# The last mixer of a three-part kernel: low parts, normalisation and the root chain placed on other engines

## Chip, cores and metric

The kernel runs on one core of a Trainium2 chip. The metric is device time of one execution in microseconds (us), taken as the median of several executions. The engines are named as the profile names them: PE (TensorE matmul, with its weight loads as PEld), DVE (VectorE), ACT (ScalarE), POOL (GpSimd) and SP (the queue that issues the DMAs).

## What is computed

The reference is a chain of three parts on a tensor of 4 batches, 768 positions and 384 features: a delta-rule attention, then a Fourier mixing with an MLP, then a gated mixer. Only the last part is touched by the change:

```python
def _moe2_ref(x, w_in, w_spatial, b_spatial, w_out):
    h = np.maximum(x @ w_in, 0.0)
    d_ff = h.shape[-1]
    u, v = (h[..., :d_ff // 2], h[..., d_ff // 2:])
    mu = np.mean(v, axis=-1, keepdims=True)
    var = np.mean((v - mu) ** 2, axis=-1, keepdims=True)
    v_n = (v - mu) / np.sqrt(var + 1e-06)
    v_s = np.einsum('ts,bsd->btd', w_spatial, v_n) + b_spatial[None, :, None]
    gated = u * v_s
    return (gated @ w_out).astype(np.float32)
```

## The kernel before, in words

Everything is float32 in and out. TensorE reads its operands as fp32r, which keeps fewer bits, so each operand is split into a high part (a rounded copy, made by ScalarE) and a low part (source minus high part). A product is then three matmuls: high by high, high by low, low by high (`PASS`).

The gated mixer is `mlp2`, and it works batch by batch, four times. In one batch:

- **Block stage.** Three blocks `kk` of positions. For each, two tiles of `v` (128 positions by 512, `v0` and `v1`, one from each half of the sequence) come from 9 matmuls each (L964); ScalarE applies the relu from PSUM (L967), VectorE takes mean and variance (L968, L969). A chain on two numbers per row (L970 to L976) makes the reciprocal of the deviation: add 1e-6, a root on ScalarE (L971), one Newton step that refines that root, a reciprocal. L978 normalises both tiles. The spatial product is done in the Winograd form of Strassen's method, seven products of half size for four, so VectorE also builds four sums of quarter tiles (L983 to L986, `S`). `operands` makes the high (L947, ScalarE) and low (L948, GpSimd) part of each: per block one of 256 elements per row and three of 512, all into the tile `A`.
- **Left halves.** Eight tiles `u` of 128 by 384, 9 matmuls each (L995), relu by ScalarE (L999). TensorE does these 72 matmuls while the block stage's last block is still being worked on.
- **Spatial products.** Seven products for each of two column halves `m`, 9 matmuls each (L1015), in a bank of PSUM each. VectorE adds their results up from PSUM (L1018 to L1034). `gate` multiplies a result by its `u` (L1002), ScalarE makes the high part (L1004), GpSimd the low part (L1005).
- **Output.** 72 matmuls with `wo` (L1043), a copy from PSUM by ScalarE (L1049), a store.
- Beside the products, the next batch is turned to its transposed form (`turn`): VectorE transposes 32x32 blocks into the scratch `x[0]` (L754), SP issues 16 small DMAs, and ScalarE and VectorE split the result (L745, L746). The scratch is one region, so the second half's L754 waits until the first half's 16 DMAs have landed.

`L964`'s tiles, the `u` tiles and the spatial products share one set of four PSUM banks, `bankX`. A bank comes free when ScalarE (L967, L999) or VectorE (L1018 to L1034) has read it.

The order on each engine isn't written by hand in this stage: a list scheduler with its own model of durations sets it when the kernel is built, and each engine then works strictly in that order. So an instruction that waits holds up everything behind it on its engine.

Of the kernel before, what the change touches and what calls it, by code (L numbers as in the profile page):

```python
# [7 lines left out]
F32 = mybir.dt.float32  # L8
F32R = mybir.dt.float32r
I32 = mybir.dt.int32  # L10
AF = mybir.ActivationFunctionType
ALU = mybir.AluOpType
AX = mybir.AxisListType
SUB, ADD, MUL, MAX = ALU.subtract, ALU.add, ALU.mult, ALU.max
# [3 lines left out]
DM = H * D  # L18
# [47 lines left out]
class Kernel:  # L66
# [863 lines left out]
    def mlp2(self, prep, x, wi, Bo, wo, bsb, A, hs, p, sm, out):  # L930
        nc = self.nc
        xs = x[0].rearrange("p t f -> p (t f)")
        vs = [xs[:, 0:DG], xs[:, DG : 2 * DG]] + [hs[:, i * DG : i * DG + DG] for i in range(4)]
        S = xs[:, 2 * DG : 4 * DG].rearrange("p (o c) -> p o c", o=4)
        tmp = [hs[:, i * DM : i * DM + DM] for i in range(6)]
        ots = [xs[:, (3 + i) * DM : (4 + i) * DM] for i in range(3)]

        gl = [A[:, 0, o].rearrange("p h k c -> p (h k c)") for o in (0, 3, 4, 1)]
        bias = [bsb[:, i * DM : i * DM + DM] for i in range(2)]
        n_out = 0  # L940

        def operands(at, n, kk, src):

            o = A[:, :, at : at + n, :, kk]
            hi, lo = (o[:, :, :, i].rearrange("p m o c -> p o m c") for i in range(2))
            src = src.rearrange("p (o m c) -> p o m c", o=n, m=2)
            nc.scalar.copy(out=hi, in_=src)  # L947
            nc.gpsimd.tensor_sub(lo, src, hi.bitcast(F32))  # L948

        for b in range(B):  # L950
            for got in prep:
                pass
            xT = got
            prep = self.mlp2_prep(x[b + 1], lambda: xs[:, : 3 * DM]) if b + 1 < B else iter(())
            for kk in range(3):
                q = sm[:, kk % 2]
                st, mv = q[:, :12].rearrange("p (t n) -> p t n", t=2), q[:, 12:16].rearrange("p (t n) -> p t n", t=2)
                v, s, r = (q[:, 16 + 2 * i : 18 + 2 * i] for i in range(3))
                v0, v1 = vs[2 * kk : 2 * kk + 2]
                for t, vt in enumerate((v0, v1)):  # L960
                    pv = self.bank("h", [128, DG])
                    for c in range(3):
                        for j, (i, k) in enumerate(PASS):
                            nc.tensor.matmul(  # L964
                                pv, lhsT=xT[t][i][:, c, kk * 128 : kk * 128 + 128], rhs=wi[2 * c + 1][k], start=(c + j == 0), stop=(c == 2 and j == 2)
                            )
                    nc.scalar.activation(vt, pv, AF.Relu)  # L967
                    nc.vector.bn_stats(out=st[:, t], in_=vt)  # L968
                    nc.vector.bn_aggr(out=mv[:, t], in_=st[:, t])  # L969
                nc.vector.tensor_scalar_add(v, mv[:, :, 1], 1e-6)  # L970
                nc.scalar.sqrt(s, v)  # L971
                nc.vector.reciprocal(r, s)
                nc.vector.tensor_mul(v, v, r)
                nc.vector.tensor_add(v, v, s)
                nc.vector.tensor_scalar_mul(v, v, 0.5)
                nc.vector.reciprocal(r, v)  # L976
                for t, vt in enumerate((v0, v1)):
                    nc.vector.tensor_scalar(out=vt, in0=vt, scalar1=mv[:, t, 0:1], scalar2=r[:, t : t + 1], op0=SUB, op1=MUL)  # L978
                    if t == 0:
                        operands(0, 1, kk, v0[:, :256])  # L980
                    else:
                        operands(1, 2, kk, v1)
                nc.vector.tensor_add(S[:, 0], v0[:, 256:], v1[:, 256:])  # L983
                nc.vector.tensor_sub(S[:, 1], S[:, 0], v0[:, :256])
                nc.vector.tensor_sub(S[:, 2], v0[:, :256], v0[:, 256:])
                nc.vector.tensor_sub(S[:, 3], v1[:, :256], S[:, 1])  # L986
                for i in range(2):
                    operands(3 + 2 * i, 2, kk, xs[:, (2 + i) * DG : (3 + i) * DG])
            u, gh = {}, {}
            for hf in range(2):  # L990
                for f in range(4):
                    pu = self.bank("h", [128, DM])
                    for c in range(3):
                        for j, (i, k) in enumerate(PASS):
                            nc.tensor.matmul(  # L995
                                pu, lhsT=wi[2 * c][i][:, f * 128 : f * 128 + 128], rhs=xT[hf][k][:, c], start=(c + j == 0), stop=(c == 2 and j == 2)
                            )
                    u[hf, f] = p.tile([128, DM], F32, name=f"u{hf}{f}")
                    nc.scalar.activation(u[hf, f], pu, AF.Relu)  # L999

            def gate(g, f, hf):
                nc.vector.tensor_mul(g, g, u[hf, f])  # L1002
                gh[hf, f] = p.tile([128, DM], F32R, name=f"u{hf}{f}")
                nc.scalar.copy(out=gh[hf, f], in_=g)  # L1004
                nc.gpsimd.tensor_sub(gl[f][:, hf * DM : hf * DM + DM], g, gh[hf, f].bitcast(F32))  # L1005

            for m in range(2):
                t1, t2, t5, t3 = (tmp[i] for i in ((0, 1, 2, 3), (4, 5, 0, 1))[m])
                add = nc.vector.tensor_add

                def product(o, name):
                    acc = self.bank("h", [128, DM])
                    for kk in range(3):
                        for j, (i, k) in enumerate(PASS):
                            nc.tensor.matmul(acc, lhsT=A[:, m, o, i, kk], rhs=Bo[name, kk][:, k], start=(kk + j == 0), stop=(kk == 2 and j == 2))  # L1015
                    return acc

                add(t1, product(0, "11"), bias[0])  # L1018
                add(t2, product(4, "T2"), t1)
                add(t5, product(3, "T1"), bias[1])  # L1020
                if m:
                    got = next(prep, None) or got
                add(t1, product(1, "21"), t1)
                gate(t1, m, 0)
                add(t3, product(5, "T3"), t2)
                add(t2, t2, t5)
                add(t5, t3, t5)
                gate(t5, 2 + m, 1)
                got = next(prep, None) or got
                add(t2, product(6, "22"), t2)  # L1030
                gate(t2, m, 1)
                if m:
                    got = next(prep, None) or got
                add(t3, product(2, "T4"), t3)  # L1034
                gate(t3, 2 + m, 0)
                if m == 0:
                    got = next(prep, None) or got

            def result(po, t, hf, fs, last):
                for f in fs:  # L1040
                    for j, (i, k) in enumerate(PASS):
                        a = gl[f][:, hf * DM + t * 128 :] if i else gh[hf, f][:, t * 128 :]
                        nc.tensor.matmul(po, lhsT=a[:, :128], rhs=wo[f][k], start=(f + j == 0), stop=(f == last and j == 2))  # L1043

            def store(po, t, hf):
                nonlocal n_out
                o = ots[n_out % 3]
                n_out += 1
                nc.scalar.copy(out=o, in_=po)  # L1049
                self.load(out=out[6 * b + 3 * hf + t], in_=o)  # L1050

            po = [self.bank("o", [128, DM]) for _ in range(3)]
            for t in range(3):
                result(po[t], t, 1, (0, 2, 3), 1)
                got = next(prep, None) or got
            for t in range(3):
                result(po[t], t, 1, (1,), 1)
                store(po[t], t, 1)
            for t in range(3):
                po = self.bank("o" if t else "pz", [128, DM])  # L1060
                result(po, t, 0, (0, 2, 1, 3), 3)
                store(po, t, 0)
# [269 lines left out]
```

## Time and profile before

| | |
|---|---|
| median of 3 executions | 870.35 us (868.94 to 871.19) |
| the profiled execution, its own time | 869.52 us |
| its span from first to last instruction | 867.7 us |
| busy share: PE, DVE, ACT, POOL | 96%, 74%, 47%, 12% |
| granted TensorE clock over the span | 0.984 of full speed |
| `mlp2`: from the first L964 to the last matmul | 616.3 to 864.4 us |
| POOL instructions of L948 and L1005 | 48 and 32 |

The stage that the change touches is the last 29% of the span. There the granted clock is 1.00 throughout, TensorE is busy nearly all the time, and the useful reading is where TensorE stops and for whom. A matmul's shown duration runs past the start of the next, since matmuls overlap: work per matmul is the distance from start to start, not the duration. Idle time in brackets is what an engine had no instruction running, with the engine, tile and line that ended it.

### The profile page before, as it was taken

How to read it: one execution, taken by the hardware profiler on the slowest of the kernel's cores; microseconds unless marked ns; L12 is line 12 of the kernel's file. 1: busy time of each engine (PE TensorE's matmuls, PEld its weight loads, DVE VectorE, ACT ScalarE, POOL GpSimd, SP SyncE). 2: the span in 40 equal slices, each digit the busy share in tenths (PEclk: the TensorE clock that was granted, in tenths of full speed). 3: DMA queues.
4: the chain of work that ended last, by engine and by line, in shares of the span. 5: the costliest groups of instructions: out<-in, count | busy, mean ns of one | idle time of the engine just before them, and what ended most of it. 6: DMA issues, size and time to landing. Idle time of an engine off the chain costs nothing.

```text
span 867.7 us, 18516 instructions
## 1 busy us (share of the span) xinstructions
PE 836.4 (96%) x7147; PEld 805.1 (93%) x7147; DVE 645.0 (74%) x1828; ACT 405.0 (47%) x991; POOL 101.5 (12%) x109
## 2 busy tenths in 40 slices
PE   7979999999998899999999999999999999999998
PEld 7869999999998798999999999999989889999998
DVE  4999999998968897785664892426698487667672
ACT  1669888889765434222213352224442432423432
POOL 2000000000000000000000000000063253333351
PEclk8969999999999999999999999999999999999999
DMA  8275665533550900001022411112001101102001
GB/s 222 67 189 135 172 189 161 160 84 104 141 168 20 341 5 1 1 2 28 1 69 78 128 28 28 37 55 64 29 0 49 62 9 47 56 25 62 25 1 54
DMA packets 57675, 67.21 MB, mean 77 GB/s; under 512 B 31826, under 2 KB 48947, under 8 KB 57587
## 3 DMA queue, kind: packets, MB, share of 16 engines
q1 hardware_dynamic: 57586, 66.03, 26.4%
q8 instruction: 56, 0.92, 0.5%
q14 instruction: 33, 0.26, 0.1%
HBM read 53.62 MB, written 4.72 MB: 67 GB/s over the span
## 4 chain that ended last, share of the span: by engine, by line
PE 70%; DVE 22%; ACT 3%; DMA 2%; issue 2%; SPq 1%; POOL 0%; DVEq 0%; ACTq 0%; POOLq 0%
PE bankX L818 15%; PE bankY L831 14%; PE bankX L1015 8%; PE bankY L1043 5%; PE bankY L438 3%; PE bankY L409 3%; PE bankY L440 3%; PE bankY L425 3%; PE bankX L964 3%; PE bankX L221 2%; DVE tm L308 2%; DVE Ts L313 2%; PE bankX L637 2%; PE bankZ L380 2%; PE bankV L831 1%
## 5 line engine op out<-in xcount | busy, mean ns | idle before, releaser
L831 PE MATMUL bankY<-w,hx 128*128 128x384 f32 x756 | 149.0, 338 | 2.2 <-DVE w L720 1.2
L818 PE MATMUL bankX<-uh,w 128*128 128x384 f32 x504 | 136.2, 337 | 0.7 <-DVE ul L746 0.7
L831 PEld LDWEIGHTS bankY<-w,hx 128*128 128x128 f32 x756 | 132.3, 188 | 3.9 <-DVE w L720 1.8
L823 DVE SCALAR_TENSOR_TENSOR hx<-bankX,hx 128x384 fp32r<-128x384 f32 x84 | 46.2, 551 | 72.8 <-ACT hx L822 72.5
L822 ACT ACTIVATE hx<-bankX 128x384 fp32r<-128x384 f32 x84 | 41.2, 490 | 126.2 <-PE bankX L818 121.8
L948 POOL TENSOR_TENSOR A<-x,A 128x512 fp32r<-128x512 f32 (+1 forms) x32 | 40.2, 1277 | 485.5 <-ACT A L947 485.5
L818 PEld LDWEIGHTS bankX<-uh,w 128*128 128x128 f32 x504 | 91.6, 188 | 1.3 <-DVE ul L746 0.9
L1015 PE MATMUL bankX<-w,A 128*128 128x384 f32 x456 | 82.9, 335 | 2.7 <-ACT u L999 2.7
L818 PE MATMUL bankX<-ul,w 128*128 128x384 f32 x252 | 84.5, 335 | 0.0
L1015 PEld LDWEIGHTS bankX<-w,A 128*128 128x128 f32 x456 | 79.3, 188 | 3.6 <-ACT u L999 3.6
L438 PE MATMUL bankY<-WU,gak 128*112 128x96 f32 (+1 forms) x384 | 70.1, 271 | 2.7 <-ACT x L455 2.7
L440 PE MATMUL bankY<-Sb,cw 112*112 112x96 f32 (+1 forms) x352 | 64.2, 265 | 2.6 <-DVE cw L426 2.5
L313 DVE TENSOR_TENSOR Ts<-Ts,tm 128x110 f32<-128x110 f32 (+26 forms) x264 | 59.4, 263 | 0.9
L308 DVE TENSOR_TENSOR tm<-Ts 128x110 f32<-128x110 f32 (+26 forms) x264 | 59.0, 261 | 0.4
L438 PEld LDWEIGHTS bankY<-WU,gak 128*112 128x112 f32 (+1 forms) x384 | 52.2, 178 | 5.9 <-ACT x L455 3.4
L409 PE MATMUL bankY<-gak,TT 128*128 128x96 f32 x384 | 53.1, 284 | 4.4 <-ACT gak L402 4.0
L414 ACT COPY WU<-bankY 64x384 f32<-64x384 f32 x96 | 45.4, 473 | 21.7 <-PE bankY L409 20.3
L409 PEld LDWEIGHTS bankY<-gak,TT 128*128 128x128 f32 x384 | 49.8, 203 | 5.1 <-ACT gak L402 4.4
L440 PEld LDWEIGHTS bankY<-Sb,cw 112*112 112x112 f32 (+1 forms) x352 | 48.4, 176 | 3.9 <-issue 2.1
L995 PE MATMUL bankX<-xh,s 128*128 128x384 f32 x192 | 49.6, 336 | 0.0
L1004 ACT CAST u<-hx 128x384 fp32r<-128x384 f32 x32 | 16.0, 513 | 67.4 <-DVE hx L1002 67.4
L818 PEld LDWEIGHTS bankX<-ul,w 128*128 128x128 f32 x252 | 47.3, 188 | 0.0
(217 smaller groups left out, 1781.6 us busy)
## 6 DMA issues: line engine op xcount, KB each, us to landing
kq<-in_kq_dram SPq DMA_DIRECT2D x24, 448.0 KB, 3.9
qt<-in_qt_dram SPq DMA_DIRECT2D x48, 196.0 KB, 3.4
gak<-in_kv_dram SPq DMA_DIRECT2D x48, 192.0 KB, 3.8
w<-in_w_dram SPq DMA_DIRECT2D x24, 384.0 KB, 7.8
out_dram<-x SPq DMA_DIRECT2D x24, 192.0 KB, 1.9
kq<-in_kc_dram SPq DMA_DIRECT2D x8, 448.0 KB, 12.7
x<-x SPq DMA_DIRECT2D x96, 36.0 KB, 1.9
s<-in_wi_dram SPq DMA_DIRECT2D x6, 512.0 KB, 4.4
```

Of the source, the lines that this page charges most:

```text
L308: nc.vector.tensor_tensor(out=tm, in0=T[:, r, k : k + 1].to_broadcast(sh), in1=T[:, k : k + 1, :k].to_broadcast(sh), op=MUL)
L313: nc.vector.tensor_add(o, o, tm)
L409: nc.tensor.matmul(pb[:, hp].rearrange("p t d -> p (t d)"), lhsT=tt[:, o + hp], rhs=kv[:, hp], start=True, stop=True)
L414: nc.scalar.copy(out=o_, in_=pb[hs])
L438: nc.tensor.matmul(pd[:m, hp], lhsT=ak[:, hp, :m], rhs=u[:, hp], start=True, stop=(c == 0))
L440: nc.tensor.matmul(pd[:m, hp], lhsT=cw[:, hp, :m], rhs=sb[:, hp], start=False, stop=True)
L818: nc.tensor.matmul(ph, lhsT=w1[f][i][:, c * 128 : c * 128 + 128], rhs=cur[k][:, c], start=(c + j == 0), stop=(c == 2 and j == 2))
L823: nc.vector.scalar_tensor_tensor(out=hl, in0=ph, scalar=0.0, in1=hh.bitcast(F32), op0=MAX, op1=SUB)
L831: nc.tensor.matmul(acc[t], lhsT=hx[i][:, t * 128 : t * 128 + 128], rhs=w2[e][k], start=(e == 0 and j == 0), stop=(e == 11 and j == 2),)
L995: nc.tensor.matmul(pu, lhsT=wi[2 * c][i][:, f * 128 : f * 128 + 128], rhs=xT[hf][k][:, c], start=(c + j == 0), stop=(c == 2 and j == 2))
L1015: nc.tensor.matmul(acc, lhsT=A[:, m, o, i, kk], rhs=Bo[name, kk][:, k], start=(kk + j == 0), stop=(kk == 2 and j == 2))
L1043: nc.tensor.matmul(po, lhsT=a[:, :128], rhs=wo[f][k], start=(f + j == 0), stop=(f == last and j == 2))
```

## The change

Four edits, all in `mlp2`. Line numbers after the second edit are one higher than before, so L1015 before is L1016 after, L1004 is L1005, and so on; the normalisation is L978 before and L979 after.

```diff
@@ operands
             nc.scalar.copy(out=hi, in_=src)
-            nc.gpsimd.tensor_sub(lo, src, hi.bitcast(F32))
+            nc.vector.tensor_sub(lo, src, hi.bitcast(F32))
@@ the chain of the deviation
-                nc.vector.tensor_scalar_add(v, mv[:, :, 1], 1e-6)
+
+                nc.vector.tensor_scalar(out=v, in0=mv[:, :, 1], scalar1=1e-6, scalar2=0.25, op0=ADD, op1=MUL)
                 nc.scalar.sqrt(s, v)
                 nc.vector.reciprocal(r, s)
                 nc.vector.tensor_mul(v, v, r)
                 nc.vector.tensor_add(v, v, s)
-                nc.vector.tensor_scalar_mul(v, v, 0.5)
                 nc.vector.reciprocal(r, v)
+                nc.vector.scalar_tensor_tensor(out=s, in0=mv[:, :, 0], scalar=-1.0, in1=r, op0=MUL, op1=MUL)
                 for t, vt in enumerate((v0, v1)):
-                    nc.vector.tensor_scalar(out=vt, in0=vt, scalar1=mv[:, t, 0:1], scalar2=r[:, t : t + 1], op0=SUB, op1=MUL)
+                    nc.scalar.activation(vt, vt, AF.Identity, scale=r[:, t : t + 1], bias=s[:, t : t + 1])
@@ gate
                 nc.scalar.copy(out=gh[hf, f], in_=g)
-                nc.gpsimd.tensor_sub(gl[f][:, hf * DM : hf * DM + DM], g, gh[hf, f].bitcast(F32))
+                nc.vector.tensor_sub(gl[f][:, hf * DM : hf * DM + DM], g, gh[hf, f].bitcast(F32))
```

With a quarter of the variance under the root, the root is half the deviation, and the Newton step's sum needs no halving. The normalisation `(v - mean) * r` becomes `v * r + (-mean * r)` on ScalarE, with both factors read per row.

The scheduler orders all engines anew from the first block of the stage on. Three places show it, all in the last batch.

The first is TensorE at the start of the spatial products (`bankX_9622` is the first product, `9633` the second, and so on; in a group of nine the three blocks `kk` come in order, and `x3` covers high by high, high by low and low by high). Before:

```order
L1015 MATMUL bankX_9622<-B0_4474,A_7663 128x384 x3
L1015 MATMUL bankX_9622<-w2_4_7502,A_7663 128x384 x3
L1015 MATMUL bankX_9622<-w1_9_7626,A_7663 128x384 x3
L1015 MATMUL bankX_9633<-w2_3_7442,A_7663 128x384 x3
L1015 MATMUL bankX_9633<-w1_8_7568,A_7663 128x384 x3
L1015 MATMUL bankX_9633<-w2_10_7653,A_7663 128x384 x2
```

Now:

```order
L1016 MATMUL bankX_9622<-B0_4474,A_7663 128x384 x3
L1016 MATMUL bankX_9622<-w2_4_7502,A_7663 128x384 x3
L1016 MATMUL bankX_9633<-w2_3_7442,A_7663 128x384 x3
L1016 MATMUL bankX_9633<-w1_8_7568,A_7663 128x384 x3
L1016 MATMUL bankX_9622<-w1_9_7626,A_7663 128x384 x2
L1016 MATMUL bankX_9644<-w2_2_7414,A_7663 128x384 x3
L1016 MATMUL bankX_9644<-w1_7_7536,A_7663 128x384 x2
L1016 MATMUL bankX_9622<-w1_9_7626,A_7663 128x384
L1016 MATMUL bankX_9644<-w1_7_7536,A_7663 128x384
L1016 MATMUL bankX_9655<-w1_4_7439,A_7663 128x384 x3
L1016 MATMUL bankX_9655<-w2_6_7565,A_7663 128x384 x2
L1016 MATMUL bankX_9633<-w2_10_7653,A_7663 128x384 x2
```

The third block's operands (`w1_9`, `w2_10`) moved back behind the first two blocks of the second, third and fourth product. In the first batch the first product still stands whole, and the rest is as here.

The second place is ScalarE on the same stretch (`u_9584` to `u_9620` are the last four of the eight `u` tiles, whose banks the first four products take over; `A<-hx` are operands of the third block's own tiles, `A<-x` of its sums). Before:

```order
L999 ACTIVATE u_9572<-bankX 128x384
L947 CAST A<-hx 128x2x128
L947 CAST A<-hx 128x2x2x128
L999 ACTIVATE u_9584<-bankX 128x384
L947 CAST A<-x_61 128x2x2x128
L999 ACTIVATE u_9596<-bankX 128x384
L947 CAST A<-x_61 128x2x2x128
```

Now:

```order
L1000 ACTIVATE u_9572<-bankX 128x384
L947 CAST A<-x_61 128x2x2x128
L1000 ACTIVATE u_9584<-bankX 128x384
L1000 ACTIVATE u_9596<-bankX 128x384
L979 ACTIVATE hx<-hx,s_7670 128x512 x2
L947 CAST A<-hx 128x2x128
L1000 ACTIVATE u_9608<-bankX 128x384
L947 CAST A<-hx 128x2x2x128
L1000 ACTIVATE u_9620<-bankX 128x384
L947 CAST A<-x_61 128x2x2x128 x2
```

Two of these four relus now stand ahead of the third block's normalisation, and all four ahead of the casts of its sums. In the first batch all four stand behind the normalisation, but still ahead of the casts of the sums except the fourth.

The third place is VectorE, from the chain of the third block on to the end of the block stage. Now:

```order
L975 TENSOR_TENSOR s_7670<-s_7670 128x2
L948 TENSOR_TENSOR A<-x_61,A 128x2x2x128
L976 RECIPROCAL s_7670<-s_7670 128x2
L977 SCALAR_TENSOR_TENSOR s_7670<-s_7670 128x2
L986 TENSOR_TENSOR x_61<-hx 128x256
L984 TENSOR_TENSOR x_61<-hx 128x256
L948 TENSOR_TENSOR A<-hx,A 128x2x128
L985 TENSOR_TENSOR x_61<-x_61,hx 128x256
L987 TENSOR_TENSOR x_61<-hx,x_61 128x256
L948 TENSOR_TENSOR A<-hx,A 128x2x2x128
L948 TENSOR_TENSOR A<-x_61,A 128x2x2x128 x2
```

The low parts (L948) are VectorE's now and stand among the sums and the chain; the normalisation, which stood between L976 and the sums, is gone from this list.

## Rows read from the trace of the kernel before

**Rows 1.** The page's 40 slices of the span: busy tenths of VectorE and GpSimd.
```profile
DVE  4999999998968897785664892426698487667672
POOL 2000000000000000000000000000063253333351
```

**Rows 2.** Timeline of TensorE in `mlp2`: start, duration, instruction, count, [idle before, releaser].
```profile
631.81 0.34 PE L995 MATMUL bankX<-xh,s 128*128 128x384 f32 x1
...
644.20 0.34 PE L995 MATMUL bankX<-xh,s 128*128 128x384 f32 x1
644.99 0.79 PE L1015 MATMUL bankX<-B,A 128*128 128x384 f32 x3 [0.45 <-ACT u L999]
...
647.50 4.98 PE L1015 MATMUL bankX<-w,A 128*128 128x384 f32 x27 [0.67 <-ACT u L999]
652.32 0.68 PE L1015 MATMUL bankX<-B,A 128*128 128x384 f32 x3
...
706.34 0.79 PE L1015 MATMUL bankX<-B,A 128*128 128x384 f32 x3 [0.48 <-ACT u L999]
...
709.69 1.48 PE L1015 MATMUL bankX<-w,A 128*128 128x384 f32 x7 [1.52 <-ACT u L999]
...
784.78 0.79 PE L1043 MATMUL bankY<-s,u 128*128 128x384 f32 x3 [0.65 <-ACT u L1004]
...
828.94 0.79 PE L1015 MATMUL bankX<-B,A 128*128 128x384 f32 x3 [0.31 <-ACT u L999]
...
831.25 0.97 PE L1015 MATMUL bankX<-w,A 128*128 128x384 f32 x4 [0.47 <-ACT u L999]
```

**Rows 3.** Waits of TensorE's weight loads in `mlp2`: total, times, longest.
```profile
PEld bankX L1015 <- ACT u L999: 5.8, 6, 1.8
```

**Rows 4.** Timeline of ScalarE ahead of the last stop.
```profile
830.18 0.62 ACT L947 CAST A<-x 128x512 fp32r<-128x512 f32 x1 [1.29 <-DVE x L984]
830.71 0.48 ACT L999 ACTIVATE u<-bankX 128x384 f32<-128x384 f32 x1
```

**Rows 5.** Timelines of VectorE and GpSimd in the last batch's block stage.
```profile
811.44 0.13 DVE L973 TENSOR_TENSOR s<-s 128x2 f32<-128x2 f32 x1
...
817.97 0.69 DVE L968 BATCH_NORM_STATS2 s<-hx 128x6 f32<-128x512 f32 x1 [0.77 <-ACT hx L967]
...
818.80 1.28 DVE L973 TENSOR_TENSOR s<-s 128x2 f32<-128x2 f32 x1
...
822.15 0.42 DVE L983 TENSOR_TENSOR x<-hx 128x256 f32<-128x256 f32 x1
...
824.89 2.96 DVE L978 TENSOR_SCALAR hx<-hx,s 128x512 f32<-128x512 f32 x2
...
817.52 2.54 POOL L948 TENSOR_TENSOR A<-x,A 128x512 fp32r<-128x512 f32 x2 [2.06 <-ACT A L947]
```

**Rows 6.** Groups by line and shape: busy us, mean ns of one, idle before.
```profile
L720 DVE TENSOR_TENSOR s<-cvd,s 128x512 fp32r<-128x512 f32 x6 | 4.0, 681 | 0.0
L823 DVE SCALAR_TENSOR_TENSOR hx<-bankX,hx 128x384 fp32r<-128x384 f32 x84 | 46.2, 551 | 72.8 <-ACT hx L822 72.5
L947 ACT CAST A<-x 128x512 fp32r<-128x512 f32 x28 | 17.2, 618 | 18.9 <-DVE x L984 13.5 <-DVE s L970 3.0 <-DVE x L986 2.0
L194 ACT ACTIVATE gak<-bankX,mk 128x128 f32<-128x128 f32 x16 | 5.9, 367 | 2.3 <-PE bankX L219 1.1
L195 ACT COPY gak<-bankX 128x128 f32<-128x128 f32 x16 | 4.1, 257 | 0.0
L999 ACT ACTIVATE u<-bankX 128x384 f32<-128x384 f32 x32 | 14.8, 487 | 0.2
L978 DVE TENSOR_SCALAR x<-x,s 128x512 f32<-128x512 f32 x8 | 4.0, 544 | 0.1
```

**Rows 7.** Timeline of VectorE at the third batch's two rounds of transposes (L754).
```profile
768.54 1.50 DVE L754 STREAM_TRANSPOSE x<-x 128x384 f32<-128x384 f32 x3 [1.60 <-POOL A L948]
...
782.62 1.50 DVE L754 STREAM_TRANSPOSE x<-x 128x384 f32<-128x384 f32 x3 [3.03 <-DMA x<-x]
```

## The prediction

> **What bounds the kernel now.** I read the page first, then TensorE's timeline in `mlp2`, then the waits, then the engine that is waited for. The page says two things: GpSimd works almost only in the last quarter of the span, and VectorE is well filled there [rows 1]. So the change can only act on `mlp2`. There TensorE is the bound: the 72 matmuls of L995 in the first batch start 12.39 us apart from first to last, 0.1745 us each, without a break [rows 2]. What can be won is the time in which TensorE stops. The timeline shows seven stops: in the first batch 0.45 and 0.67 us, in the second 0.48 and 1.52, in the third 0.65, in the last 0.31 and 0.47 [rows 2]. A stop costs more than its idle time: the last matmul ahead of it is shown for 0.34 us but only keeps TensorE for 0.1745, and the first group of three after it takes 0.79 us where it takes 0.68 elsewhere [rows 2]. So each stop is its idle time plus 0.17 plus 0.11. The seven add up to 4.55 + 7 x 0.28 = 6.5 us, and the six ahead of L1015 alone to 3.90 + 1.68 = 5.6 us. This is nearly all that any edit of this stage can win.
>
> Why does it stop? All six wait for ScalarE's relu of a `u` tile, L999; the weight loads say the same [rows 2, 3]. That relu isn't slow (0.49 us, [rows 6]); it is late, since it stands behind the casts of L947, and those wait for VectorE's sums: the cast ahead of the last stop had waited 1.29 us for L984, and the relu follows it at once [rows 4]. A product needs a bank that this relu frees. So the true cause is VectorE at the end of the block stage. And VectorE is late there because its instructions are stretched: the two-number product L973 takes 0.13 us in one place and 1.28 in another, where it ends together with GpSimd's pair of low parts; the two normalisations take 2.96 us where a single one takes 0.544 undisturbed [rows 5, 6].
>
> **The change part by part.**
>
> *Low parts to VectorE.* Added on VectorE per batch in the block stage: 9 of 512 elements at 0.681 and 3 of 256 at 0.42, by the undisturbed rows of the same kind (L720 and L983) [rows 5, 6], 7.4 us. Removed: 6 normalisations at 0.544, 3.3 us. So 4.1 us more of nominal work, against a stretch that goes: in the last batch's third block alone 1.15 us at L973 and about 1.9 at the normalisations. At worst these two cancel; which end lies nearer decides the path, so I lay it out below. In the gate stage 8 low parts of 384 are added at 0.551 [rows 6], 4.4 us per batch, likewise against stretch that goes.
>
> *The normalisation to ScalarE.* No row has this form: 512 elements with scale and bias both read per row. Below, the plain copy of 512 from SBUF takes 0.618 us; and one factor read per row costs 0.110 (L194 takes 367 ns, L195 on the same shape without it 257) [rows 6]. I take 0.618 + 2 x 0.11 = 0.84 us, with 0.62 and 1.0 as the ends. Per batch ScalarE gets 6 x 0.84 = 5.0 us. The rule that speaks against this is in the Trainium skill, page "ScalarE: Activation LUTs": its "Rules for kernel authors" leave multiplies and adds to VectorE, and its section "What ACT_TABLE_LOAD costs" charges about 93 ns for each factor read per row, which would make it about 0.80 us, an estimate; for one factor the rows agree (110 ns), for two none shows it. By either figure the pair stays inside the margins below, so the sum is the same.
>
> *The chain.* One instruction removed, one of the same small kind added behind the reciprocal: nothing.
>
> *The path, in the order of the listing.* Zero is the last L964 of a batch; L995 then covers 72 x 0.1745 = 12.5 us, and the first product could start at 12.5. In the last batch of before zero is 828.94 - 0.31 - 0.34 - 71 x 0.1745 = 815.9, and the last statistic ended at 818.66, +2.75 [rows 2, 5]; I take +2.9, since it now stands behind one more low part. From it to L977 VectorE's list has six low parts of 512 and one of 256, five sums at 0.42 and seven small ones at about 0.17: 4.1 + 0.4 + 2.1 + 1.2 = 7.8 us, all back to back, since ScalarE's side of each is ready earlier. So the factors of the third block stand at +10.7. ScalarE: pair to +12.4, cast, relu of `u12` to +13.4, cast, relu of `u13` to +14.5, the two casts of sums to +15.7. VectorE beside it: two sums, the low part of the first operand at +13.7, its last low part at +16.5. TensorE's claims, counted in matmuls from 12.5: bank of `u10` at +12.5, freed near +10 since its relu stands ahead of the pair; bank of `u12` after 14 matmuls, +14.9; low part of the first product's third block after 19, +15.8; bank of `u13` after 21, +16.2; high parts of the sums after 26, +17.0 (first cast +15.1), low after 31, +17.9. Each claim is met with 1 to 2 us to spare, in batches two to four.
>
> In the first batch the four relus stand behind the pair. There L977 of the third block waits behind L986 for the second block's pair and comes at about +6.6; the pair ends at +8.5, and five casts and a relu later `u10` is done at about +12.1, against 12.5. The margin is 0.4 us: at 1.0 us per normalisation it is gone, and 0.3 us of the first batch's 1.7 would stay.
>
> *What is late next.* VectorE's adds from PSUM. They now start at +16.5, in batches two and three behind three transposes of 1.50 us together [rows 7], so the first add ends at +18.5; the fifth product claims that bank after 36 matmuls, at +18.8. Tight, but met. The second round of transposes waits for 16 DMAs, 12.6 us after the first round's end (770.04 to 782.62) [rows 7]. In before this held VectorE for 3.03 us and made the third batch's stop of 0.65 [rows 2, 7]. Now the first round ends at +18, the second could start at +30.6, and in the new order it stands four adds later, behind the third add of the second half, which ends at +29: VectorE waits 1.6 us instead of 3.0, with the remaining banks already free. I count this stop (0.93 us with its 0.28) as gone.
>
> **The sum.** All seven stops: 6.5 us. I leave 0.3 us for the first batch's thin margin and 0.2 for new short ones: a gain of 6.0. The profiled execution took 869.52 us, the span and 1.8 us around it; the change would make it 863.5. The median of the three runs lies 0.8 us above the profiled one, so the median becomes **864.3 us**.
>
> **The rivals.**
>
> *ScalarE becomes the late one.* The pair L979 is in place on the path and the relus and casts queue behind it. If the chain's end slips by 2 us (VectorE's low parts waiting for casts that wait for normalisations), batches two to four stop again at `u12`, and the first at `u10`: four stops of about 0.6 + 0.28, 3.5 us given back. Gain 2.5, time 867.8. For: ScalarE was the releaser of every stop. Against: half of the relus were moved ahead of the pair, and the margins. Chance 0.15.
>
> *The low parts of the gate hold the adds up: slower.* Each L1006 waits for ScalarE's cast, about 0.65 us with its handovers, and stands in VectorE's one list ahead of adds that free banks. Up to the last of them its list from +16.5 on has 34 instructions of 0.551, two rounds of transposes (3.0), three low parts of the next batch (1.7) and the DMA wait (1.6): 25.0 us, done at +41.5. TensorE asks for it after 126 matmuls of L1016, 45 of L1044 and 7 of L964, at +43.6 at the earliest. So 2.1 us per batch are spare; all eight waits exposed would be 5.2 us, 3.1 late in each of the three batches with transposes, 9.3 us given against 6.5 gained: 873. It turns slower than before once more than 4.3 us per batch are exposed, seven of the eight. Against: in the order other work stands between most L1003 and their L1006, and TensorE's last claims can slide. For: in the tail of the second half three low parts stand close behind their gates. Chance 0.08.
>
> *The stretch isn't GpSimd's.* Then VectorE keeps its slow instructions and gets 4.1 + 4.4 us more per batch; with 2 us spare in either stage that is 4 x 4.5 = 18 us lost, 888. The paired end in the two timelines [rows 5] speaks against it. Chance 0.02.
>
> *Nothing won:* the six stops go and others of the same size come, since the scheduler's own durations made this order as well as the old one. 870, chance 0.05.
>
> **How the numbers follow.** The forecast has the remaining 0.70, with a range of its own of 862.8 (all stops gone, no new ones) to 866. A measurement of this kernel tells about 0.3% from no change, so faster means below 867.7. Faster: 0.70 and two thirds of the first rival, 0.80. The same: the rest of it, the last rival and a little of the second, 0.12. Slower: 0.08. The range takes the runs' spread of 0.5 us below the best case and the first rival above: 862.3 to 867.9.
>
> **What would show it.** Right: no idle ahead of L1016 with L1000 as its releaser; L973 to L975 at 0.2 us throughout; L948 on VectorE at 0.68 and L979 near 0.84; VectorE's busy time in `mlp2` hardly changed, ScalarE's up by 20 us. Wrong: stops ahead of L1016 or L1044 with VectorE as the releaser (the second rival), or still L1000 behind L979 (the first), or L979 well above 1.0 us.

## The result, and the profile after

| | before | after |
|---|---|---|
| median | 870.35 us (868.94 to 871.19, 4 executions) | 862.39 us (861.20 to 863.37, 4 executions) |
| ratio, with its 95% interval | 1 | 0.991 (0.989 to 0.9929) |
| the profiled execution, its own time | 869.52 us | 863.37 us |
| `mlp2`: first L964 to the end of the last matmul | 616.28 to 864.35: 248.07 us | 617.46 to 858.16: 240.70 us |

The change made the kernel faster by 8.0 us between the medians. The stage that it touches became 7.37 us shorter; the two profiled executions differ by only 6.15 us because the part ahead, which the change leaves alone, took 1.18 us longer in the second one. Over all profiled executions of this study that part ended between 614.55 and 619.32 us, so from here on the **length of the stage** is the finer measure.

The page's 40 slices of the kernel after answer to [rows 1]:

```profile
DVE  5999999998968798685573795436678378476563
...
POOL 2000000000000000000000000000000000000000
```

GpSimd has left the last quarter. TensorE's timeline around the four starts of the spatial products (start, duration, instruction, count) answers to [rows 2]:

```profile
645.37 0.34 PE L996 MATMUL bankX<-xh,s 128*128 128x384 f32 x1
645.54 0.68 PE L1016 MATMUL bankX<-B,A 128*128 128x384 f32 x3
646.07 5.88 PE L1016 MATMUL bankX<-w,A 128*128 128x384 f32 x33
...
704.89 0.68 PE L1016 MATMUL bankX<-B,A 128*128 128x384 f32 x3
...
764.24 0.68 PE L1016 MATMUL bankX<-B,A 128*128 128x384 f32 x3
...
823.58 0.68 PE L1016 MATMUL bankX<-B,A 128*128 128x384 f32 x3
```

No row has a bracket any more, in the whole stage: TensorE never waits. The first group takes 0.68 us in each batch, where it took 0.79 behind a stop, and the batches start 59.35 us apart instead of some 61.3. The view of the weight loads' waits, which held 5.8 us for ScalarE's relu [rows 3], has no row left.

Groups by line and shape in `mlp2` after (busy us, mean ns of one | idle before), against [rows 5, 6]:

```profile
L948 DVE TENSOR_TENSOR A<-x,A 128x512 fp32r<-128x512 f32 x28 | 18.9, 683 | 1.8 <-ACT A L947 1.6
L1006 DVE TENSOR_TENSOR A<-hx,u 128x384 fp32r<-128x384 f32 x32 | 17.2, 552 | 0.1
...
L948 DVE TENSOR_TENSOR A<-hx,A 128x256 fp32r<-128x256 f32 x8 | 3.4, 422 | 0.0
...
L974 DVE TENSOR_TENSOR s<-s 128x2 f32<-128x2 f32 x12 | 1.8, 149 | 0.0
...
L979 ACT ACTIVATE hx<-hx,s 128x512 f32<-128x512 f32 x16 | 12.5, 811 | 0.0
...
L979 ACT ACTIVATE x<-x,s 128x512 f32<-128x512 f32 x8 | 6.0, 806 | 0.0
```

The low parts take the 0.68, 0.42 and 0.55 us that rows of the same kind had shown, and L974, the old L973 that took 0.13 or 1.28 us [rows 5], is at 0.149 in the mean. Last, the busy time of each engine from 616 to 868 us, first before, then after (`sum` is the whole stretch; `mean` is of the four parts in which it was read):

```profile
sum 252.00, PE 243.69 PEld 231.20 DVE 172.29 ACT 90.16 POOL 93.97; mean PE 60.92 PEld 57.80 DVE 43.07 ACT 22.54 POOL 23.49
```

```profile
sum 252.00, PE 242.16 PEld 232.87 DVE 160.01 ACT 105.93 POOL 0.00; mean PE 60.54 PEld 58.22 DVE 40.00 ACT 26.48 POOL 0.00
```

VectorE took over all of GpSimd's work, and was busy 12.3 us less. It gained 46.7 us of low parts (the four groups of L948 and that of L1006) and lost 24 normalisations of 0.544, 13 us. So about 46 us of its busy time before was stretch.

### The profile page after: what moved, and what is told of

The parts are those of the page before. It is cut to its first block, busy times and chain, and to the rows that moved or that the text cites. A ratio compares the mean times of both kernels' runs of the same rounds, so it can differ in the third digit from the quotient of the medians.

```text
span 861.6 us, 18463 instructions
## 1 busy us (share of the span) xinstructions
PE 833.8 (97%) x7147; PEld 805.2 (93%) x7147; DVE 632.2 (73%) x1884; ACT 420.4 (49%) x1015; POOL 7.5 (1%) x29
## 4 chain that ended last, share of the span: by engine, by line
PE 82%; DVE 13%; ACT 2%; DMA 2%; issue 1%; POOL 0%; SPq 0%; DVEq 0%; ACTq 0%; POOLq 0%
PE bankX L818 15%; PE bankY L831 14%; PE bankX L1016 10%; PE bankX L996 6%; PE bankX L964 6%; PE bankY L1044 5%; PE bankY L438 4%; PE bankY L409 3%; PE bankY L440 3%; PE bankY L425 3%; PE bankX L221 2%; PE bankZ L380 2%; DVE tm L308 2%; DVE Ts L313 2%; PE bankX L637 2%; PE bankV L831 1%
## 5 line engine op out<-in xcount | busy, mean ns | idle before, releaser
L1016 PE MATMUL bankX<-w,A 128*128 128x384 f32 x456 | 81.7, 334 | 0.0
L1016 PEld LDWEIGHTS bankX<-w,A 128*128 128x128 f32 x456 | 79.4, 188 | 0.0
L996 PE MATMUL bankX<-xh,s 128*128 128x384 f32 x192 | 49.6, 336 | 0.0
L1005 ACT CAST u<-hx 128x384 fp32r<-128x384 f32 x32 | 15.8, 513 | 66.6 <-DVE hx L1003 66.6
L425 PE MATMUL bankY<-gak,WU 128*112 128x112 f32 x352 | 45.8, 276 | 0.0
## 6 DMA issues: line engine op xcount, KB each, us to landing
kq<-in_kc_dram SPq DMA_DIRECT2D x8, 448.0 KB, 14.5
```

What stands on the lines that cost most here:

```text
L425: nc.tensor.matmul(pc[:, hp], lhsT=w[:, hp], rhs=gas[bc][:, hp, : C + D], start=True, stop=True)
L996: nc.tensor.matmul(pu, lhsT=wi[2 * c][i][:, f * 128 : f * 128 + 128], rhs=xT[hf][k][:, c], start=(c + j == 0), stop=(c == 2 and j == 2))
```

## The experiments

Two theories stood at first. **Theory 1**: GpSimd's low parts stretch VectorE's instructions in the block stage, so that its sums, ScalarE's casts, the relus behind them and the banks come late; the move of the low parts is the gain. **Theory 2**: the gain is VectorE's relief from the normalisation, and the new order that comes with it. The later runs ask which low parts, and what it is in GpSimd's work that stretches. All medians below stand beside before's, run on the same chip.

**e1, the low parts alone.** The kernel before with L948 and L1005 on VectorE; normalisation and chain stay.

```diff
-            nc.gpsimd.tensor_sub(lo, src, hi.bitcast(F32))
+            nc.vector.tensor_sub(lo, src, hi.bitcast(F32))
...
-                nc.gpsimd.tensor_sub(gl[f][:, hf * DM : hf * DM + DM], g, gh[hf, f].bitcast(F32))
+                nc.vector.tensor_sub(gl[f][:, hf * DM : hf * DM + DM], g, gh[hf, f].bitcast(F32))
```

> Low parts on VectorE as in the change, normalisation and root chain as before. Theory 1 (GpSimd's low parts stretch VectorE's instructions, and that made TensorE stop): no stretched instruction is left, so at most a small part of the gain is missing. VectorE has 3.3 us more per batch than with the change, against margins of 1 to 2 us, so 0 to 1 us of stops per batch come back: 862.5 to 866 us. Theory 2 (the gain comes from the normalisation leaving VectorE and the order that the scheduler makes of it): 868 us or more.

Measured: 863.00 us (862.19 to 864.91), ratio 0.9923 (0.9906 to 0.994). The stage lasts 240.73 us and TensorE's timeline has no stop in it. The low parts alone give the whole gain.

**e2, the rest alone.** The kernel after with both low parts back on GpSimd, so that the normalisation on ScalarE and the half roots are what differs from before.

```diff
-            nc.vector.tensor_sub(lo, src, hi.bitcast(F32))
+            nc.gpsimd.tensor_sub(lo, src, hi.bitcast(F32))
...
-                nc.vector.tensor_sub(gl[f][:, hf * DM : hf * DM + DM], g, gh[hf, f].bitcast(F32))
+                nc.gpsimd.tensor_sub(gl[f][:, hf * DM : hf * DM + DM], g, gh[hf, f].bitcast(F32))
```

> Normalisation on ScalarE and the half roots as in the change, low parts on GpSimd as before. Theory 1: GpSimd still stretches VectorE (two-number products of over 1 us, sums of over 0.8 us), the casts come as late as before, and ScalarE has 5 us more per batch: 868.5 to 873 us. Theory 2: most of the gain is there, 862.5 to 865 us.

Measured: 869.21 us (866.34 to 870.81), ratio 0.999 (0.9979 to 1.0001), the stage 246.24 us. TensorE stops four times, now ahead of `u` tiles:

```profile
647.91 0.44 PE L996 MATMUL bankX<-xh,s 128*128 128x384 f32 x1 [2.11 <-ACT u L1000]
...
708.39 0.44 PE L996 MATMUL bankX<-xh,s 128*128 128x384 f32 x1 [0.76 <-ACT u L1000]
...
768.75 0.44 PE L996 MATMUL bankX<-xh,s 128*128 128x384 f32 x1 [0.76 <-ACT u L1000]
...
829.13 0.44 PE L996 MATMUL bankX<-xh,s 128*128 128x384 f32 x1 [0.76 <-ACT u L1000]
```

With the 0.28 us that each stop costs beside its idle time these are 4.39 + 1.12 = 5.5 us, as much as the stage is longer than after's. The groups of the same run show the chain behind it, VectorE's instructions stretched as before:

```profile
L948 POOL TENSOR_TENSOR A<-x,A 128x512 fp32r<-128x512 f32 x28 | 37.8, 1372 | 0.3 <-ACT A L947 0.3
...
L987 DVE TENSOR_TENSOR x<-hx,x 128x256 f32<-128x256 f32 x8 | 9.2, 1154 | 0.0
...
L975 DVE TENSOR_TENSOR s<-s 128x2 f32<-128x2 f32 x12 | 7.3, 609 | 0.2
```

Theory 2 falls: with the normalisation off VectorE and GpSimd still beside it, the median can't be told from before's. The stage of this one profile is 1.8 us shorter than before's 248.07, so something of the other edits and their order may be left while GpSimd reads, a quarter of the change's 7.4 us, but the runs' scatter is as large.

**e6, the old root chain** in the kernel after: `tensor_scalar_add` of 1e-6, and the separate halving ahead of the reciprocal.

```diff
-                nc.vector.tensor_scalar(out=v, in0=mv[:, :, 1], scalar1=1e-6, scalar2=0.25, op0=ADD, op1=MUL)
+                nc.vector.tensor_scalar_add(v, mv[:, :, 1], 1e-6)
...
+                nc.vector.tensor_scalar_mul(v, v, 0.5)
```

> The change with the root chain of before (halving as an instruction of its own), everything else as changed; the scheduler makes a somewhat other order of it. Both theories: 12 more small instructions of about 0.17 us, inside margins of 1 us and more, so the time of the change, 861.5 to 863.5 us. A third theory, that the shorter chain decides: 865 us or more.

Measured: 863.00 us (861.49 to 865.24), ratio 0.9916 (0.9899 to 0.9934), the stage 240.70 us without a stop. The half roots are worth nothing that shows.

**e3 and e4, which low parts.** The kernel after with one of the two places back on GpSimd: in e3 the gate's (L1006), in e4 the block stage's (L948), each by the one line shown in e2.

> The change, but the gate's low parts back on GpSimd; those of the block stage on VectorE. If the block stage alone made TensorE stop (six of the seven stops of before stood there), the stage's stops stay away but for the two or three short ones at the output matmuls: 862 to 865 us, and a two-input sum of the gate (before 0.8 to 0.9 us) is stretched again without a price. If the gate's share counts as much: 866 us or more.

> The change, but the block stage's low parts back on GpSimd; those of the gate on VectorE. If the block stage is the place, the stops come back as with all low parts on GpSimd: 867 to 871 us. If the gate counts as much: 866 us or less.

Measured: e3 861.86 us (861.42 to 863.84), ratio 0.9907 (0.9891 to 0.9923), the stage 240.60 us, no stop. e4 869.81 us (867.14 to 870.88), ratio 0.9995 (0.998 to 1.0009), the stage 248.20 us. e3 came out 0.1 us below the range that was expected, e4 inside its own. Of the 7.5 us that e4's stage is longer than after's, the four stops (2.11, 0.82, 1.07 and 0.82 us idle, and 0.28 each) are 5.9, about as much as in e2; the other 1.6 are matmuls at a lower clock behind the first stop (see the last section). That e4 comes as near to before's 248.07 as it does is therefore in part chance. In e3 VectorE's instructions of the gate are stretched, to 0.76 from 0.552 us, and it costs nothing:

```profile
L1006 POOL TENSOR_TENSOR A<-hx,u 128x384 fp32r<-128x384 f32 x32 | 35.3, 1124 | 614.5 <-ACT u L1005 601.5 <-issue 13.0
L1003 DVE TENSOR_TENSOR hx<-hx,u 128x384 f32<-128x384 f32 x32 | 23.7, 759 | 0.3
...
L1027 DVE TENSOR_TENSOR hx<-hx 128x384 f32<-128x384 f32 x8 | 7.2, 898 | 0.2
...
L1020 DVE TENSOR_TENSOR hx<-bankX,hx 128x384 f32<-128x384 f32 x8 | 4.5, 558 | 9.2 <-PE bankX L1016 9.2
```

L1027 adds two tiles of SBUF, which holds the program's tiles, L1020 one of SBUF to a result of TensorE in PSUM. Of the eight of each, five of L1027 run beside a low part of GpSimd and take 1.05 to 1.17 us, the other three 0.55; four of L1020 run beside one, and all eight take 0.56.

So only the block stage's low parts matter. The first batch of e4 shows the whole path, GpSimd, VectorE and ScalarE in turn:

```profile
639.44 1.29 POOL L948 TENSOR_TENSOR A<-hx,A 128x512 fp32r<-128x512 f32 x1 [0.15 <-ACT A L947]
640.70 2.79 POOL L948 TENSOR_TENSOR A<-x,A 128x512 fp32r<-128x512 f32 x2
```

```profile
639.50 1.26 DVE L974 TENSOR_TENSOR s<-s 128x2 f32<-128x2 f32 x1
...
641.01 1.25 DVE L975 TENSOR_TENSOR s<-s 128x2 f32<-128x2 f32 x1
...
642.50 1.01 DVE L977 SCALAR_TENSOR_TENSOR s<-s 128x2 f32<-128x2 f32 x1
```

```profile
643.54 1.52 ACT L979 ACTIVATE hx<-hx,s 128x512 f32<-128x512 f32 x2 [1.79 <-DVE s L977]
644.96 0.47 ACT L1000 ACTIVATE u<-bankX 128x384 f32<-128x384 f32 x1
```

Three instructions on two numbers per row, 0.15 us each where nothing disturbs them, take 3.5 us, and each ends within 0.03 us of one of GpSimd's three low parts; ScalarE waits 1.79 for the last of them, its relu stands behind, and TensorE stops 2.11 us for the relu, at 645.49.

**e5, GpSimd's reading given back.** The kernel after, and beside its low parts 84 subtractions on GpSimd whose result nothing reads, of 256 elements from SBUF. The order on TensorE, VectorE and ScalarE is that of the kernel after.

```diff
             nc.vector.tensor_sub(lo, src, hi.bitcast(F32))
+            for j in range(n):
+                h = hi[:, j].bitcast(F32)
+                nc.gpsimd.tensor_sub(self.idn.bitcast(mybir.dt.bfloat16).rearrange("p (m c) -> p m c", m=2), h, h)
```

> The change, with GpSimd also subtracting each high part of the block stage from itself into a spare tile that nobody reads: 84 instructions of 256 elements, some 0.8 us each. The order on TensorE, VectorE and ScalarE is the same, and none of them waits for GpSimd except where a high part is rewritten a batch later. Theory 1: VectorE's two-input instructions in the block stage are stretched again (means of 0.6 us and more for the two-number products), VectorE falls behind and TensorE stops ahead of L1016 or L1044: 865 to 869 us. Theory 2: the same time as the change, 861.5 to 863.5 us.

Measured: 878.78 us (875.14 to 880.67), ratio 1.0096 (1.0073 to 1.012), the stage 253.66 us, 13.0 longer than after's. The sign was expected, the size was not. VectorE and GpSimd on the second batch:

```profile
699.11 0.83 DVE L948 TENSOR_TENSOR A<-hx,A 128x256 fp32r<-128x256 f32 x1
...
700.62 1.10 DVE L948 TENSOR_TENSOR A<-x,A 128x512 fp32r<-128x512 f32 x1
701.64 0.83 DVE L988 TENSOR_TENSOR x<-x,hx 128x256 f32<-128x256 f32 x1
```

```profile
696.74 8.73 POOL L951 TENSOR_TENSOR idn<-A 128x256 bf16<-128x256 f32 x10 [0.87 <-POOL idn L951]
```

Each of VectorE's instructions here has two inputs in SBUF, and each takes about 0.41 us more, whatever its own length: 0.83 for 0.42, 1.10 for 0.68. GpSimd's own take 0.61 us at the shortest and 0.94 where they meet VectorE's low parts of 512. So the two engines seem to take turns rather than to share, and VectorE pays for nearly every one of GpSimd's instructions that it meets. In all its busy time rises by 27.0 us, to 186.97, and TensorE stops for VectorE's own products:

```profile
710.12 3.61 PE L1019 MATMUL bankX<-w,A 128*128 128x384 f32 x19 [0.85 <-ACT A L947]
714.16 1.15 PE L1019 MATMUL bankX<-w,A 128*128 128x384 f32 x5 [0.44 <-DVE A L948]
717.03 0.79 PE L1019 MATMUL bankX<-B,A 128*128 128x384 f32 x3 [1.72 <-DVE hx L1022]
```

That it is worse than before fits with VectorE doing the low parts here and paying for GpSimd's turns as well (186.97 us busy against before's 172.29); no run takes the two apart.

**e7, GpSimd busy without reading.** The same places as in e5, but each subtraction is a one-element copy (so that it starts when its tile is there) and four memsets of 128 by 128.

```diff
             nc.vector.tensor_sub(lo, src, hi.bitcast(F32))
+            for j in range(n):
+                nc.gpsimd.tensor_copy(out=self.idn[:, :1], in_=hi[:, j, 0, :1].bitcast(F32))
+                for _ in range(4):
+                    nc.gpsimd.memset(self.idn, 0.0)
```

> The change, with GpSimd kept busy at the same places as in the run with the unused subtraction, but by 336 memsets of 128 elements (0.2 us each, some 76 us in all) and 84 copies of one element: hardly any reading of the scratchpad memory by GpSimd. Same order on TensorE, VectorE and ScalarE. If it is GpSimd's reading that holds VectorE's two-input instructions up: low parts stay near 0.68 us and the time is that of the change, 861.5 to 864 us. If any work of GpSimd does: 870 us or more, near the run with the subtraction.

Measured: 864.20 us (861.40 to 864.97), ratio 0.9919 (0.9897 to 0.994), the stage 240.70 us without a stop; the median lies 0.2 us above the first theory's range, far from the second's.

```profile
L952 POOL MEMSET idn<- 128x128 f32 x336 | 69.2, 206 | 19.4
L950 POOL COPY idn<-A 128x1 f32<-128x1 f32 x84 | 26.7, 318 | 530.2 <-ACT A L947 434.9 <-issue 89.5 <-POOL idn L952 0.9
L948 DVE TENSOR_TENSOR A<-x,A 128x512 fp32r<-128x512 f32 x28 | 18.8, 681 | 1.8 <-ACT A L947 1.6
```

GpSimd is busy for 95.9 us, as long as in before, and VectorE's low parts stay at 0.681 us. What stretches is GpSimd's reading of whole tiles, not its being busy, nor its writes. The Trainium skill states this, page "SBUF — State Buffer", section "Who interferes with whom": a VectorE instruction with two SBUF inputs contends with a GpSimd instruction that reads SBUF, and not with one that only writes it. The runs agree: about +0.41 us an instruction in e5, none in e7.

**e8, the gate's margin.** The kernel after with 64 unused subtractions of 192 elements on GpSimd beside the gate's low parts, the order unchanged, to see how much the gate can bear on VectorE.

```diff
                 nc.vector.tensor_sub(gl[f][:, hf * DM : hf * DM + DM], g, gh[hf, f].bitcast(F32))
+                for j in range(2):
+                    h = gh[hf, f][:, j * 192 : j * 192 + 192].bitcast(F32)
+                    nc.gpsimd.tensor_sub(self.idn.bitcast(mybir.dt.bfloat16)[:, :192], h, h)
```

> The change, with GpSimd also subtracting each high part of the gate from itself (64 instructions of 192 elements, some 0.65 us each) into a tile that nobody reads; same order on the other engines. By my sum the gate has some 2 us per batch to spare in the first three batches; 8 x 1.3 us of GpSimd per batch stretch VectorE by 4 to 6 us, so 2 to 4 us of stops in each of three batches: 866 to 874 us. If the gate has more to spare than I summed: 862 to 865 us.

Measured: 862.54 us (861.90 to 864.31), ratio 0.9913 (0.9898 to 0.9929), the stage 240.70 us without a stop.

```profile
L1006 DVE TENSOR_TENSOR A<-hx,u 128x384 fp32r<-128x384 f32 x32 | 24.0, 765 | 0.0
L1003 DVE TENSOR_TENSOR hx<-hx,u 128x384 f32<-128x384 f32 x32 | 20.3, 654 | 0.2
...
L1030 DVE TENSOR_TENSOR hx<-hx 128x384 f32<-128x384 f32 x8 | 5.9, 735 | 0.1
```

Against 552 to 555 ns in the kernel after, these three groups cost VectorE 32 x 0.213 + 32 x 0.102 + 8 x 0.18 = 11.5 us more, 2.9 in each batch, and no stop follows. The stops that were expected from the prediction's 2.1 us did not come: the gate has more to spare than that sum left.

**e9, one line.** The kernel before with the block stage's low parts on VectorE, and nothing else: the first of the two lines of e1.

> The kernel before with one edit alone: the low parts of the block stage (L948) on VectorE; the normalisation, the chain and the gate's low parts stay as they were. Theory 1 (GpSimd's reading beside VectorE in the block stage is the whole cause; the other three edits are worth nothing): no stop of TensorE ahead of L1015, the stage lasts 240.7 us as in the change, median 861.5 to 864.5. Rival (the gate's low parts or the normalisation's move take a share that the earlier runs hid, since each of them left two of the three edits in): some stops remain, the stage lasts 242 to 246 us, 864.5 to 868.

Measured: 862.51 us (860.28 to 862.96), ratio 0.9911 (0.9894 to 0.9927); the stage lasts from 614.55 to 855.13, 240.58 us, without a stop. One line of the four edits, with the order that the scheduler makes of it, is the whole gain. The gate's low parts on GpSimd stretch L1002 there to 0.746 us, at no cost.

**What the order has to do with it.** Every placement that was built has an order of its own on TensorE; only e5, e7 and e8 keep that of the kernel after. So one could think that the gain lies in the orders. Three kernels have the block stage's low parts on GpSimd (before, e2, e4), in three orders, and each stops; five have them on VectorE with no such reading beside it (after, e1, e3, e6, e9), in five orders, and none does; and e5 brings stops back with the order unchanged, where e7 does not. So GpSimd's reading in the block stage is the cause. What before's own order would cost without that reading no run shows.

No kernel of the study is faster than the one after by more than the runs' scatter. In seven of them (after, e1, e3, e6, e7, e8, e9) the stage takes 240.6 to 240.7 us: TensorE without a stop, which is as far as a placement on the other engines can bring it.

## Why the prediction was right, and where its sizes were off

**The cause and its path** were right: the stops went, all seven, and the chain from GpSimd over VectorE's two-number products, ScalarE's queue and the bank to TensorE is what e4's rows show and what e1, e2 and e9 tell apart. One row was put in the wrong place: the L973 of 1.28 us at 818.80 belongs to the second block's chain (the third's begins with its L970 at 820.01). It stood between the third block's statistic and the third block's chain, so it held up the same path.

**The gain in the stage** was forecast as 6.0 us and is 7.4. Two terms make the difference. The seven stops are worth 6.5 us, as the sum had it, but the 0.5 us that I left for the first batch's margin and for new short stops wasn't needed. And three short waits of 0.18 to 0.24 us at 678.34, 726.44 and 786.79 in the trace of before, 0.9 us with what follows each, have no bracket in the timeline, and I had not counted them. The other 0.6 of the 8.0 us between the medians lies within the scatter of the part ahead. The predicted 864.3 is 1.9 us above the measured 862.39. That this is still inside the range, by 0.1 us, owes something to luck: it is below the forecast's own range, which began at 862.8 for "all stops gone, no new ones", and the sum gives 870.35 - 6.5 = 863.85 for that case. The bound was about 1 us lower than its working, and the three waits that were not counted filled that microsecond.

**The margins** were summed too tight, in two ways. I added durations: VectorE's and ScalarE's instructions start before the one ahead has ended, so a list is as long as the distances from start to start. And I kept before's time for the third block's last statistic, +2.75 and a little. In before its relu stood behind a cast that had waited 2.18 us for VectorE (L947 at 816.82); after, the statistic ended at 812.89, +1.9. The last batch after, VectorE's end of the block stage and ScalarE beside it:

```profile
815.11 0.42 DVE L948 TENSOR_TENSOR A<-hx,A 128x256 fp32r<-128x256 f32 x1
815.45 0.42 DVE L984 TENSOR_TENSOR x<-hx 128x256 f32<-128x256 f32 x1
815.78 0.69 DVE L948 TENSOR_TENSOR A<-x,A 128x512 fp32r<-128x512 f32 x1
816.39 0.42 DVE L985 TENSOR_TENSOR x<-x,hx 128x256 f32<-128x256 f32 x1
...
819.72 0.16 DVE L977 SCALAR_TENSOR_TENSOR s<-s 128x2 f32<-128x2 f32 x1
...
824.82 1.29 DVE L948 TENSOR_TENSOR A<-x,A 128x512 fp32r<-128x512 f32 x2
```

```profile
821.03 1.51 ACT L979 ACTIVATE hx<-hx,s 128x512 f32<-128x512 f32 x2
822.45 0.39 ACT L947 CAST A<-hx 128x256 fp32r<-128x256 f32 x1
822.74 0.48 ACT L1000 ACTIVATE u<-bankX 128x384 f32<-128x384 f32 x1
...
823.78 0.49 ACT L1000 ACTIVATE u<-bankX 128x384 f32<-128x384 f32 x1
```

A low part of 512 shows 0.68 to 0.69 us and holds VectorE for 0.61; one of 256 shows 0.42 and holds it for 0.34. From the batch's first L996 at 811.02 (72 matmuls ahead of 823.58), the factors stood at +8.9 instead of +10.7 (1.0 us of this by the earlier statistic, 0.8 by the overlap, net of a wait of 0.46 for a cast), the pair L979 was done at +11.5 instead of +12.4, the two relus at +12.2 and +13.2 instead of +13.4 and +14.5, the last low part at +15.1 instead of +16.5. In the first batch the relu that I saw done at +12.1, 0.4 us ahead of its claim, was done at about +10.6. So each claim had one to two us more than the sum gave it, and the first rival, ScalarE as the late one, was further off than 0.15.

**The normalisation on ScalarE** takes 0.806 to 0.811 us, where I took 0.84. The move is worth nothing that the medians show, by e2 while GpSimd is beside it, and by e9 against the kernel after once it is gone. The estimate of 0.80 by the Trainium skill's page "ScalarE: Activation LUTs", section "What ACT_TABLE_LOAD costs", was the nearer one. The "Rules for kernel authors" of the same page of the Trainium skill, which leave such work to VectorE, decided nothing here.

**The transposes.** The 1.6 us that VectorE would still wait for the scratch's 16 DMAs did not come. VectorE came to the second round at 780.51, +28.8, as I had it (+29), and found the scratch free: this is 12.3 us after the first round's end, so the DMAs had landed sooner than the 12.6 us that I took from before. There SP issued the sixteenth 10.3 us after the first, here 9.4. That the stop of 0.65 there goes was right.

**The gate** had more to spare than the 2.1 us of the sum, by e8 at least 2.9. The reason is again the overlap: 34 instructions of 0.551 start 0.47 apart (L1006 at 773.31, L1028 at 773.77, L1031 at 774.24), 2.8 us less than I counted. TensorE also asks 0.4 us later than I had it, since the seven matmuls of L964 stand 0.23 us apart (805.75, 805.98, 806.21) and not 0.1745. The slower rival needed 4.3 us exposed per batch, and its chance of 0.08 rested on too tight a sum.

**Busy times.** VectorE's was to change hardly and fell by 12.3 us: the stretch, some 46 us, was larger than I had seen from one batch's rows. ScalarE's was to rise by 20 and rose by 15.8; the pair's two groups show 18.5 us, and the rest is overlap: the durations of all its instructions sum up to 19.4 us more, which is L979's alone.

**What would have shown it wrong** did not come: no stop ahead of L1016 or L1044, and L979 below 1.0 us.

## What to carry to other kernels

Work that is put on GpSimd to relieve VectorE is not free to VectorE: here it read whole tiles from SBUF, VectorE's instructions that read two tiles there had to wait, and the profile showed it as two-number instructions that took up to 1.3 us, ending together with GpSimd's. Look for such pairs first in the stage whose last releaser is late, and move only that work: one line in the block stage gave everything, and the same line in the gate nothing. When margins are summed, add distances from start to start, not durations, on every engine.

## What the runs showed of the hardware that was not expected

**A toll that goes by GpSimd's instruction.** GpSimd's unused subtraction of 256 elements cost most of VectorE's two-input instructions that met it the same 0.41 us (e5), whether they had 256 or 512 elements. Beside GpSimd's low parts of 512 it is more: 0.9 to 1.1 us for the three small instructions of e4 above, which take 0.15 undisturbed. So a tiny instruction can pay as much as a long one (0.57 for 0.15 us at L977 in e5), and in a chain of them it adds up. It isn't only those with two inputs: the addition and scaling by constants of two numbers per row (L974 in e5) takes 0.57 instead of 0.17 us each of the three times that it meets one, while the statistics L971 and the reciprocals L976, with one input too, keep 0.68 and 0.15. Adds with one of two inputs in PSUM paid no toll (e3). And 336 memsets and 84 tiny copies cost nothing at all (e7).

**The clock after a stop.** In e4 and in e2 TensorE stops for the same 2.11 us ahead of the same instruction. In e2 the matmuls go on 0.1745 apart. In e4 nine of them stand 0.32 apart. The rows give a stretch, its length, busy time and count of PE, PEld, DVE, ACT and POOL, then the granted clock, the DMA share and GB/s; first e4, then e2, each for the stretch behind the stop:

```profile
645.50:649.30 3.80, 3.80 (x14) 3.80 (x15) 2.81 (x4) 2.95 (x8) 3.44 (x3) 0.58 0.00 0
```

```profile
647.90:652.00 4.10, 4.08 (x23) 4.09 (x24) 2.88 (x5) 3.24 (x8) 3.71 (x4) 1.00 0.00 0
```

The mean of 0.58 in e4 means that most of those 3.8 us lay at the lower of the two levels, 1.2 GHz; the mean of 1.00 in e2 is the higher one, 2.4 GHz. The slow matmuls cost e4 nine times 0.146 and two times about 0.12, 1.6 us, most of the 1.96 us by which its stage is longer than e2's. Why the clock fell after the one stop and not after the other no run here tells.
